# Top-k attention and two experts on one core: the softmax normaliser moved to GpSimd, a value product over two tiles, and all weight conversions of the second expert inside attention

## The chip, the core and the metric

The kernel runs on one core of a Trainium2 chip. The core has a matrix engine (TensorE, in the rows PE; PEld is its weight load), a vector engine (VectorE, DVE), a scalar engine (ScalarE, ACT), GpSimd (POOL), and SyncE (SP), whose queue issues every DMA of this kernel. On-chip memory is SBUF, and PSUM for what TensorE writes. Each engine runs its own instructions in the order in which they were written; engines wait for each other on semaphores. The metric is the device time of one execution in microseconds (us).

## What is computed

Attention over 4 batches, 8 heads, 576 positions and head size 64 keeps only the 32 highest scores of each row; its output goes through a gated expert and then a second one.

```python
def _attn_ref(q, k, v):                          # (4, 8, 576, 64)
    scores = scale * np.matmul(q, k.transpose(0, 1, 3, 2))
    kth = np.partition(scores, -32, axis=-1)[..., -32:-31]
    scores = np.where(scores >= kth, scores, -1e9)
    attn = np.exp(scores - np.max(scores, axis=-1, keepdims=True))
    attn = attn / (np.sum(attn, axis=-1, keepdims=True) + 1e-09)
    return np.matmul(attn, v)

def _moe_ref(x, w_gate, w_val, w_out):           # 2304 x 512, d_ff 1536
    g = x @ w_gate
    return (g * (1 / (1 + np.exp(-g))) * (x @ w_val)) @ w_out

def _moe2_ref(x, w_in, w_out):                   # d_ff 2048
    h = x @ w_in
    return (h * np.cos(h)) @ w_out
```

## The kernel before

**Tiling.** The 2304 tokens are 18 tiles of 128. They go in ten chunks c: chunks 0 and 1 of one tile, chunks 2 to 9 of two (`SIZES`). The heads go in four pairs p. A unit is one tile t of one head h: 144 units, in the order of chunk, pair, tile, head. A tile that crosses a batch boundary (tiles 4 and 13) has two segments of 64 rows with different keys and values.

**A unit (`unit_proc`).** TensorE makes 128x576 scores in PSUM (`sc`, L605), ScalarE copies them to a tile `s` (L610), VectorE finds the 32 largest by four rounds of a maximum of eight (`MAX8`, L633) and three of striking them out (`MATCH_REPLACE8`, L636). GpSimd makes two bounds from them (`b`, L647 and L651), ScalarE masks (L664) and takes the exponential with its row sum (`e`, `sm`, L675). The tile `s` stays taken until the masking is done; there are five (ring `r_s`).

**A pair of heads (`pair_proc`, `group_proc`).** TensorE transposes the exponentials of a tile's two heads (`tp`, L697), ScalarE copies them to `pt` (L702), and TensorE multiplies them with the values into `av`: one product with the tail of the values (L735) and eight with 64-column weights (L738), in full fp32, two records for each. That is done for each tile by itself. Value tiles `V` come by DMA (L568); there are three.

**The normaliser (`x_proc`).** When the row sums of a chunk and a pair of heads are there, VectorE adds 1e-9 (L759) and takes the reciprocal (L757), GpSimd spreads it (`rx`, L765), TensorE turns it (L777), ScalarE copies it and the value product, GpSimd multiplies them, and the chunk's input to the first expert is split in two fp32r parts `xh` and `xl`.

**The first expert.** For each chunk 12 blocks f of 128 hidden columns: `gv` = x times the gate and value weights (L884; for chunks 0 and 1 in plain fp32 with the operands turned, L973), silu on ScalarE and GpSimd, `y` = times the output weights (L1096), stored to DRAM. The last chunk's products are called `gvl`.

**Weights.** They come as 64-bit words, and `convert` makes fp32 of them: three ScalarE passes (L213, L216, L220), a join on VectorE (L223), an add on GpSimd (L226). The first expert's weights are then split into two fp32r parts (`w1_rest`, L300 and L303). Of the second expert's 16 blocks, 12 are converted during attention in halves (`w2_early_proc`) and stored to DRAM (`w2d`); the other four are loaded raw and converted after attention (`w2_proc`, tiles `w2s` and `cy`). All 16 are split when the first expert's weights give their room free (L1241, L1245).

**The second expert.** For 6 blocks j of 384 tokens and 16 blocks f: `h` (L1309, 12 products), its cosine product on ScalarE and VectorE, `o` (L1373, 9 products).

**What sets the order.** A planner (`Plan`) runs the steps as processes with a cost and a due time each and emits every engine's instructions in the order in which it would start them. A ring is a set of buffers: a step waits until the buffer that it reuses is free. So a changed cost or due time moves instructions all over the program.

## Time and profile before

| | us |
|---|---|
| median of 3 runs (lowest, highest) | 1283.73 (1279.42, 1286.16) |
| profiled execution | 1285.8 |
| its span | 1284.0 |
| TensorE busy | 1199.9 (93%) |
| VectorE busy | 1014.5 (79%) |
| ScalarE busy | 963.7 (75%) |
| GpSimd busy | 626.6 (49%) |

The profile is of one execution. Its span runs from the first to the last instruction; the profiled time has 1.8 us around it. Attention and the first expert take the time to about 800 us, the rest of the last chunk's first expert to about 870 us, the second expert the time from about 860 us to the end. The view of stretches gives each engine's busy time in a stretch, the timeline gives instructions with their start and length, the view of waits says who waited for whom, and the chain of waits goes back from the last instruction.

### The profile page before, as it was taken

Reading aid. Unit: us, or ns where it says so; the run is one execution under the profiler, and the core shown is the slowest. Engines: PE = TensorE matmul, PEld = TensorE weight load, DVE = VectorE, ACT = ScalarE, POOL = GpSimd, SP = SyncE. Lnnn points to the kernel's source line nnn. Section 1 sums busy time; section 2 is a strip of 40 time slices with the busy share of each in tenths; the row PEclk is TensorE's granted clock in tenths of the full one; section 3 lists DMA queues with packets and bytes.
Section 4 is the critical chain, followed back from the end, with each engine's and each line's share of the span. In section 5 each row is a group of like instructions: output and inputs, shape, how many; then the busy total and the mean of one; then the engine's idle time right before and its main releaser. Section 6 shows DMA issues by size and latency. Waiting matters only on the chain.

```text
span 1284.0 us, 24500 instructions
## 1 busy us (share of the span) xinstructions
PE 1199.9 (93%) x8544; PEld 1092.0 (85%) x8544; DVE 1014.5 (79%) x2024; ACT 963.7 (75%) x2164; POOL 626.6 (49%) x1039
## 2 busy tenths in 40 slices
PE   2588988999999999999999999998999999999998
PEld 1466765899998999999999999996999899899897
DVE  6999999999999999999999995256555555555554
ACT  6999999879898888888888877459554555455554
POOL 5556688978677767667666655456010101000000
PEclk9999989999999999999999999999999999999999
DMA  6553545555465654455545432784010101010000
GB/s 214 188 197 102 174 125 163 162 176 195 153 191 175 183 171 157 156 162 169 169 144 177 140 117 67 244 274 129 7 50 1 50 1 44 7 37 2 3 23 25
DMA packets 83099, 157.97 MB, mean 123 GB/s; under 512 B 16672, under 2 KB 35104, under 8 KB 82976
## 3 DMA queue, kind: packets, MB, share of 16 engines
q1 hardware_dynamic: 82976, 156.41, 38.3%
q8 instruction: 67, 1.10, 0.4%
q14 instruction: 56, 0.46, 0.1%
HBM read 131.20 MB, written 25.17 MB: 122 GB/s over the span
## 4 chain that ended last, share of the span: by engine, by line
PE 64%; DVE 12%; ACT 11%; DMA 5%; POOL 3%; issue 3%; SPq 1%; POOLq 0%; ACTq 0%; DVEq 0%
PE o L1373 15%; PE h L1309 15%; PE gv L884 11%; PE y L1096 8%; DVE m L633 6%; DVE w L636 5%; PE av L738 4%; PE sc L605 3%; PE tp L697 3%; PE gv L973 3%; DMA wo<-wo 1%; ACT pt L702 1%; PE gvl L884 1%; DMA y<-yo 1%; ACT s L610 1%
## 5 line engine op out<-in xcount | busy, mean ns | idle before, releaser
L633 DVE MAX8 m<-w 128x8 f32<-128x576 f32 x432 | 311.0, 745 | 1.2
L884 PE MATMUL gv<-xh,w 128*128 128x256 f32 x1344 | 289.1, 292 | 5.9 <-ACT hg L852 5.8
L884 PEld LDWEIGHTS gv<-xh,w 128*128 128x128 f32 x1344 | 224.4, 190 | 11.8 <-ACT hg L852 7.9
L1309 PE MATMUL h<-x2h,w 128*128 128x384 f32 x768 | 213.1, 338 | 4.8 <-DVE g L1343 4.8
L636 DVE MATCH_REPLACE8 w<-m,w 128x576 f32<-128x576 f32 x288 | 212.6, 739 | 0.0
L1373 PE MATMUL o<-w,gh 128*128 128x512 f32 x576 | 195.9, 395 | 0.0
L884 PE MATMUL gv<-xl,w 128*128 128x256 f32 x672 | 189.6, 282 | 0.0
L1096 PE MATMUL y<-gh,wo 128*128 128x256 f32 x768 | 159.2, 289 | 1.2 <-DMA wo<-wo 1.2
L605 PE MATMUL sc<-K,q 128*128 128x288 f32 (+1 forms) x640 | 126.6, 327 | 34.0 <-ACT s L610 14.6
L1309 PEld LDWEIGHTS h<-x2h,w 128*128 128x128 f32 x768 | 140.4, 188 | 11.1 <-DVE g L1343 7.0
L1276 POOL TENSOR_TENSOR x2l<-x,x2h 128x384 fp32r<-128x384 f32 x24 | 25.6, 1066 | 250.0 <-ACT x2h L1265 250.0
L1343 DVE TENSOR_TENSOR g<-r,h 128x384 f32<-128x384 f32 x96 | 53.2, 554 | 114.4 <-ACT r L1338 114.4
L605 PEld LDWEIGHTS sc<-K,q 128*128 128x128 f32 (+1 forms) x640 | 97.2, 197 | 44.9 <-ACT s L610 16.8
L1336 ACT ACTIVATE r<-r 128x384 f32<-128x384 f32 x96 | 50.4, 525 | 110.3 <-DVE r L1333 110.3
L702 ACT ACTIVATE pt<-tp 128x512 f32<-128x512 f32 (+1 forms) x216 | 107.1, 496 | 33.5 <-PE tp L697 32.3
L697 PE MATMUL tp<-ident,e 128*128 128x128 f32 x648 | 111.8, 283 | 21.8 <-ACT pt L702 18.1
L1096 PEld LDWEIGHTS y<-gh,wo 128*128 128x128 f32 x768 | 126.3, 190 | 5.7 <-issue 4.5
L1309 PE MATMUL h<-x2l,w 128*128 128x384 f32 x384 | 129.3, 337 | 0.0
L884 PEld LDWEIGHTS gv<-xl,w 128*128 128x128 f32 x672 | 127.9, 190 | 0.0
L1373 PEld LDWEIGHTS o<-w,gh 128*128 128x128 f32 x576 | 108.1, 188 | 21.0
L675 ACT ACTIVATE e<-e,b 128x576 f32<-128x576 f32 x144 | 112.9, 784 | 3.2 <-POOL b L651 1.4
L633 DVE MAX8 m<-s 128x8 f32<-128x576 f32 x144 | 107.3, 746 | 9.4 <-ACT s L610 6.2
(122 smaller groups left out, 2895.3 us busy)
## 6 DMA issues: line engine op xcount, KB each, us to landing
wo<-wo SPq DMA_DIRECT2D x96, 512.0 KB, 3.8
w_raw<-in_w SPq DMA_DIRECT2D x48, 512.0 KB, 4.8
V<-in_vP SPq DMA_DIRECT2D x52, 256.0 KB, 3.4
kx<-in_kT SPq DMA_DIRECT2D x64, 144.0 KB, 3.0
qx<-in_qT SPq DMA_DIRECT2D x64, 128.0 KB, 2.9
wo<-in_wo SPq DMA_DIRECT2D x12, 512.0 KB, 4.0
wo<-wo SPq DMA_DIRECT2D x24, 256.0 KB, 2.8
w2d<-c SPq DMA_DIRECT2D x24, 256.0 KB, 2.6
```

The source lines that it names most:

```text
L605: nc.tensor.matmul(sc[:r1, s, :HALF], q[:, a, t * 128:t * 128 + r1], k[:, s * HALF:s * HALF + HALF], start=a == 0, stop=a == 1)
L633: nc.vector.max(out=st["m"][:, 8 * i:8 * i + 8], in_=st["w"] if i else st["s"])
L636: nc.vector.match_replace(out=st["w"], in_to_replace=st["m"][:, 8 * i:8 * i + 8], in_values=st["w"] if i else st["s"], imm_value=LOWEST)
L675: nc.scalar.activation(st["e"], st["e"], AF.Exp, bias=st["b"][:, 2:3], scale=1.0, accum_out=smT[c, p][:, j:j + 1])
L697: nc.tensor.transpose(st["ps"][:, j - j0], e[:, j * 128:j * 128 + 128], ident)
L702: lambda: nc.scalar.activation(ptT[c, p, t][:, j0:j1], st["ps"][:, :j1 - j0], AF.Copy),
L738: nc.tensor.matmul(o[64 * h:64 * h + 64, r0:r1], m[:, j, h], pt[:, 5 * h + j, r0:r1], start=False, stop=j == 3)
L884: nc.tensor.matmul(gv[g], W1[f, kk // 2][:, a, g, kk % 2], m[:, kk], start=kk == 0 and i == 0, stop=kk == KT - 1 and i == 2)
L1096: nc.tensor.matmul(y1p[d // 2][:, d % 2], w[:, a, d * 128:d * 128 + 128], m, start=f == 0 and i == 0 and d % 2 == 0, stop=f == NF1 - 1 and ...
L1309: nc.tensor.matmul(st["h"], w[:, a, kk * 128:kk * 128 + 128], m[:, kk], start=kk == 0 and n == 0, stop=kk == KT - 1 and n == 2)
L1343: nc.vector.tensor_mul(st["g"], r, h)
L1373: nc.tensor.matmul(o[t], a[:, cs], W2[f, 1][:, m], start=f == 0 and n == 0, stop=f == NF2 - 1 and n == 2)
```

## The change

1. The normaliser's add and reciprocal go from VectorE to GpSimd. The reciprocal becomes a power of -1.
2. The value product is made once for a chunk's two tiles and a pair of heads (`av_proc`): `pt` is 256 columns wide for both tiles, and one product runs over 256 columns (or over 64 and 192 where a batch boundary lies in the chunk).
3. All 16 blocks of the second expert are converted during attention; those after attention go. `w2_proc` only loads and splits.
4. The splitting of the first expert's weights has an earlier due time (`W1S_FIRST` 96 for 122). Score tiles go from five to four, value tiles from three to two, tiles for the second expert's loaded weights (`cvx`) from five to nine.
5. The first 12 products `h` get a third PSUM bank, wait for their half of a weight block alone, and the first token block's input is due 50 us earlier.
6. Some of the planner's costs change: a strike 0.725 for 0.669 us, a transpose 0.108 for 0.09, the value product by the number of segments and tiles.

The code for turned chunks also gets branches for a last chunk of one tile; here the last chunk has two, so no instruction comes from them, and they are left out below.

```diff
-    NV = 3
+    NV = 2
-    W1S_FIRST, W1S_STEP = 122.0, 2.6
+    W1S_FIRST, W1S_STEP = 96.0, 2.7
...
     def w2_early_proc(i):
         f, half = divmod(i, 2)
-        due = due_unit(46 + 3.8 * i)
+        due = due_unit(44 + 2.9 * i)
...
-    r_s, r_sc, r_w, r_e, r_pt, r_tp, r_av = Ring(5), Ring(1), Ring(2), Ring(2), Ring(1), Ring(1), Ring(1)
+    r_s, r_sc, r_w, r_e, r_pt, r_tp, r_av = Ring(4), Ring(1), Ring(2), Ring(2), Ring(1), Ring(1), Ring(1)
...
-                yield "DVE", 0.669, strike, due, True
+                yield "DVE", 0.725, strike, due, True
...
-        end = yield "PE", 0.02 + 0.09 * (j1 - j0), turn, due, True
+        end = yield "PE", 0.02 + 0.108 * (j1 - j0), turn, due, True
...
-            ptT[c, p, t] = att.tile([128, 9, 128], F32, tag="pt", name="pt", bufs=r_pt.n)
+            if (c, p) not in ptT:
+                ptT[c, p] = att.tile([128, 9, CH], F32, tag="pt", name="pt", bufs=r_pt.n)[:, :, :SIZES[c] * 128]
...
+    def av_proc(c, p):
+        n = SIZES[c]
+        yield ev_pt[c, p]
+        segs = segments(FIRST[c], n)
+        for b, r0, r1 in segs:
+            yield ev_v[c, p, b]
+        yield r_av.gate(c * NP + p)
...
             for b, r0, r1 in segs:
                 m, tail = V[c, p, b]
-                nc.tensor.matmul(o[:, r0:r1], tail, pt[:, 4, r0:r1], start=True, stop=False)
+                nc.tensor.matmul(av[:, r0:r1], tail, pt[:, 4, r0:r1], start=True, stop=False)
                 for j in range(4):
                     for h in range(2):
-                        nc.tensor.matmul(o[64 * h:64 * h + 64, r0:r1], m[:, j, h], pt[:, 5 * h + j, r0:r1],
+                        nc.tensor.matmul(av[64 * h:64 * h + 64, r0:r1], m[:, j, h], pt[:, 5 * h + j, r0:r1],
                                          start=False, stop=j == 3)
-        end = yield "PE", 1.1, attv, due_unit(u) + 15.0, True
+        end = yield "PE", 0.34 * len(segs) + 1.13 * n, attv, due_unit(unit_of[c, p, n - 1, 1]) + 15.0, True
...
         def rinv():
             sm = smT[c, p]
-            nc.vector.reciprocal(sm, sm)
-
-        yield ("DVE", 0.07, lambda: nc.vector.tensor_scalar(smT[c, p], smT[c, p], 1e-9, None, op0=OP.add), due,
+            nc.gpsimd.tensor_tensor(sm, sm, cst[:, 2:2 + 2 * n], op=OP.pow)
+
+        yield ("POOL", 0.15, lambda: nc.gpsimd.tensor_scalar(smT[c, p], smT[c, p], 1e-9, None, op0=OP.add), due,
                True)
-        yield "DVE", 0.1, rinv, due, True
+        yield "POOL", 0.2, rinv, due, True
...
-    r_raw2, r_cvx2, r_x2, r_x2s = Ring(2), Ring(5), Ring(2), Ring(2)
+    r_cvx2, r_x2, r_x2s = Ring(9), Ring(2), Ring(2)
+    r_hc = Ring(1)
...
     def w2_proc(i):
...
-        if f < NS2:
-            yield w2_stored[f]
-            yield r_cvx2.gate(i)
...
-        else:
-            pc = pools["pbc"]
...
-            joined, t = yield from convert(
-                st["raw"].bitcast(I32), due, [r_cy2.gate(n)],
-                lambda: pools["psB"].tile([128, DM], I32, tag="cy", name="cy", bufs=r_cy2.n), into)
...
+        yield w2_stored[f]
+        yield r_cvx2.gate(i)
+
+        def load():
+            st["x"] = pools["pbc"].tile([128, DM], F32, tag="cvx", name="cvx", bufs=r_cvx2.n)
+            nc.sync.dma_start(st["x"], w2d[f, :, half * DM:half * DM + DM])
...
-        due = b_due(j, 0) - 25.0
+        due = b_due(j, 0) - (25.0 if j else 75.0)
...
-        yield ev_w2[f]
+        yield ev_w2[f, 0]
         yield ev_x2[j]
-        second = k >= H_ONE and k % 2
+        if k < H_ONE:
+            second, third, i = False, k % 3 == 2, k // 3 if k % 3 == 2 else k // 3 * 2 + k % 3
...
+                elif third:
+                    st["h"] = pools["psB"].tile([128, DM], F32, tag="h", name="h")[:, :CB]
...
-    for i in range(2 * NS2):
+    for i in range(2 * NF2):
         plan.start(w2_early_proc(i))
```

How the order of instructions changes is shown at three places, in which a name after an arrow is what is read. The first is the normaliser of chunk 6, head pair 1 (`sm` holds the row sums, `b` a unit's bounds, `rx` the spread normaliser, `gl` a part of the first expert). On VectorE before, its add and reciprocal stand between the selections of two units:

```order
L633 MAX m<-w 128x8
L759 TENSOR_SCALAR sm<-sm 128x4
L636 MATCH_REPLACE w<-m,s 128x576
L636 MATCH_REPLACE w<-m,w 128x576
L757 RECIPROCAL sm<-sm 128x4
L633 MAX m<-w 128x8 x2
```

On GpSimd now, both stand between a unit's bounds and the spread:

```order
L941 TENSOR_TENSOR vv<-th,vv 128x256
L651 TENSOR_TENSOR b_6723<-b_6723 128x1
L763 TENSOR_SCALAR sm<-sm 128x4
L761 TENSOR_TENSOR sm<-sm,cst 128x4
L951 TENSOR_TENSOR gl_6743<-vv,gh_6742 128x256
L769 TENSOR_SCALAR rx<-sm 128x256
L647 TENSOR_TENSOR b_6803<-m,cst 128x2
```

The two steps left VectorE and stand on GpSimd ahead of the next unit's bounds. The second place is TensorE at a value product of the same chunk (`gv` belongs to the first expert). Before, for one tile:

```order
L884 MATMUL gv_100<-xh,w_3_1991 128x256
L735 MATMUL av<-pt,vtail_105 128x128
L738 MATMUL av<-pt,V 64x128 x8
L884 MATMUL gv_100<-xh,w_3_1991 128x256
L884 MATMUL gv_100<-xl,w_3_1991 128x256
```

Now, for both tiles, right behind the turned normaliser:

```order
L781 MATMUL tp<-ident,rx 128x128 x2
L740 MATMUL av<-pt,vtail_107 128x256
L743 MATMUL av<-pt,V 64x256 x8
L889 MATMUL gv_100<-xh,w_5_1833 128x256
L889 MATMUL gv_100<-xl,w_5_1833 128x256
```

Two narrow blocks became one wide block. The third place is TensorE where the second expert's first products `h` stand among the last chunk's `gvl`; the number behind `w_` is the block f of the first expert. Before:

```order
L884 MATMUL gvl<-xl,w_10_2488 128x256
L884 MATMUL gvl<-xh,w_10_2488 128x256
L1309 MATMUL h<-x2h,w_0_11689 128x384
L1309 MATMUL h<-x2l,w_0_11689 128x384
L1309 MATMUL h<-x2h,w_0_11689 128x384
L884 MATMUL gvl<-xh,w_11_2541 128x256
```

Now:

```order
L889 MATMUL gvl<-xl,w_5_1833 128x256
L889 MATMUL gvl<-xh,w_5_1833 128x256
L1363 MATMUL h<-x2h,w_0_11495 128x384
L1363 MATMUL h<-x2l,w_0_11495 128x384
L1363 MATMUL h<-x2h,w_0_11495 128x384
L889 MATMUL gvl<-xh,w_6_1870 128x256
```

The first `h` moved from behind block 10 to behind block 5 of the last chunk.

## Rows read from the trace of the kernel before

**Rows 1.** Stretches: start:end, length, busy us (instructions), TensorE's granted clock, DMA share

```profile
core 0: us, PE busy (x) PEld busy (x) DVE busy (x) ACT busy (x) POOL busy (x), PEclk, DMA share, GB/s
100.00:200.00 100.00, 89.98 (x529) 66.56 (x528) 99.34 (x209) 96.11 (x222) 69.87 (x115) 0.95 0.44 136
200.00:240.00 40.00, 33.12 (x255) 25.28 (x253) 40.00 (x85) 35.97 (x80) 36.06 (x49) 1.00 0.51 157
240.00:790.00 550.00, 538.72 (x4842) 517.78 (x4841) 538.00 (x1115) 473.23 (x1139) 389.56 (x707) 1.00 0.51 161
840.00:905.00 65.00, 58.24 (x380) 53.12 (x379) 41.29 (x63) 48.53 (x99) 37.84 (x30) 1.00 0.55 181
905.00:1284.00 379.00, 375.32 (x1875) 338.43 (x1874) 198.73 (x357) 201.64 (x390) 16.26 (x16) 1.00 0.06 20
```

**Rows 2.** Timeline: start, length, engine, line; copy and first maximum, units 30 and 48

```profile
181.32 0.69 ACT L610 ACTIVATE s<-sc 128x576 f32<-128x576 f32 x1
...
187.01 0.74 DVE L633 MAX8 m<-s 128x8 f32<-128x576 f32 x1
...
278.08 0.65 ACT L610 ACTIVATE s<-sc 128x576 f32<-128x576 f32 x1
...
278.83 0.76 DVE L633 MAX8 m<-s 128x8 f32<-128x576 f32 x1
```

**Rows 3.** Waits of VectorE, 240 to 790 us: total us, times, longest

```profile
DVE m L633 <- ACT s L610: 5.7, 9, 1.5
DVE m L633 <- POOL th L935: 2.9, 2, 1.9
```

**Rows 4.** VectorE's timeline at a normaliser; then L759's durations (ns min/median/max)

```profile
503.75 0.47 DVE L759 TENSOR_SCALAR sm<-sm 128x4 f32<-128x4 f32 x1
504.13 0.08 DVE L636 MATCH_VALUE_LOAD w<-m,s 128x8 f32 x1
...
505.59 0.16 DVE L757 RECIPROCAL sm<-sm 128x4 f32<-128x4 f32 x1
505.67 0.72 DVE L633 MAX8 m<-w 128x8 f32<-128x576 f32 x1
...
L759 DVE TENSOR_SCALAR sm<-sm x40: 139/388/1319, 34.9 to 793.4; 128x4 f32<-128x4 f32 x32, 128x2 f32<-128x2 f32 x8
```

**Rows 5.** Groups of GpSimd: count | busy us, mean ns | idle before, releasers

```profile
L647 POOL TENSOR_TENSOR b<-m,cst 128x2 f32<-128x2 f32 x144 | 30.1, 210 | 86.5 <-DVE m L633 71.0 <-DVE sm L757 7.5 <-DVE sm L759 4.8
```

**Rows 6.** Line 223, the joins from 260 to 760 us: ns min/median/max, first, last

```profile
L223 DVE SCALAR_TENSOR_TENSOR w_raw<-w_raw,c x24: 658/846/1651, 262.9 to 736.0; 128x512 int32<-128x512 int32 x24
```

**Rows 7.** TensorE's timeline at a whole and at a cut value product

```profile
504.30 0.38 PE L735 MATMUL av<-pt,vtail 128*128 128x128 f32 x2
504.61 1.09 PE L738 MATMUL av<-pt,V 128*64 128x128 f32 x16
505.64 0.39 PE L884 MATMUL gv<-xh,w 128*128 128x256 f32 x1
...
581.16 0.33 PE L735 MATMUL av<-pt,vtail 128*128 128x64 f32 x2
...
583.02 0.38 PE L1096 MATMUL y<-gh,wo 128*128 128x256 f32 x1
```

**Rows 8.** Chain of waits near 100 us: start, us, what

```profile
98.53 4.99 PE gv L973 x22
103.51 0.44 PE tp L697 x4
```

**Rows 9.** Waits of SyncE's queue, whole span: total us, times, longest

```profile
SPq L568 <- PE av L738: 74.8, 29, 7.8
```

**Rows 10.** Chain of waits, one of the passes between 866 and 898 us

```profile
890.82 0.56 ACT w2s L216
```

**Rows 11.** Waits of TensorE, 790 to 905 us

```profile
PE h L1309 <- DVE g L1343: 4.8, 5, 2.7
```

**Rows 12.** Line 633, the maxima: ns min/median/max, start of the first and last

```profile
L633 DVE MAX8 m<-w x432: 722/744/765, 15.6 to 788.4; 128x8 f32<-128x576 f32 x144
```

More of the change, by code (lines that the diff above doesn't have):

```diff
@@ L32 @@
 NCH = len(SIZES)
-TURNED = [c < PLAIN for c in range(NCH)]
+TURNED = [n == 1 for n in SIZES]
 FIRST = [sum(SIZES[:c]) for c in range(NCH)]
@@ L963, in turned_gemm_proc @@
         due = moe_due(c, 2 * fp)
+        last = c == NCH - 1
         if fp:
@@ L994, in turned_gemm_proc, with tiles @@
-        ring.free(i, end, plan)
-        th, hg, vv = st["th"], st["hg"], st["vv"]
-        yield ("POOL", 0.37,
-               lambda: nc.gpsimd.tensor_scalar(th, th, 1.0, 0.5, op0=OP.add, op1=OP.mult), due, True)
-        yield "POOL", 0.69, lambda: nc.gpsimd.tensor_mul(th, th, hg), due, True
-        end = yield "POOL", 0.69, lambda: nc.gpsimd.tensor_mul(vv, th, vv), due, True
+        gate, val = bank[:, :, 0], bank[:, :, 1]
+        def tiles(*names):
+            for name in names:
+                st[name] = moe.tile([128, CH], F32, tag=name, name=name, bufs=(r_vv if name == "vv" else r_th).n)
@@ new lines, in tanh, with silu, product @@
+        def tanh():
+            tiles("th")
+            nc.scalar.activation(two("th"), gate, AF.Tanh, scale=0.5)
+        def evac():
+            tiles("hg", "vv")
+            nc.scalar.activation(two("hg"), gate, AF.Copy)
+            nc.scalar.activation(two("vv"), val, AF.Copy)
+        def silu():
+            tiles("vv")
+            nc.vector.scalar_tensor_tensor(two("vv"), two("th"), 1.0, gate, op0=OP.add, op1=OP.mult)
+        def product():
+            nc.vector.scalar_tensor_tensor(two("vv"), two("vv"), 0.5, val, op0=OP.mult, op1=OP.mult)
@@ L1000, in turned_gemm_proc @@
+        vv = st["vv"]
         r_th.free(k, end, plan)
[L1001 removed]
+        stored = not last and fp < NG0
         if not stored:
[L1003 to L1009 removed]
+            yield r_g.gate(G0[c] + (fp if last else fp - NG0))
+        if last:
+            yield r_gt.gate(fp)
+        else:
+            kt = tp_count[0]
+            tp_count[0] += 1
+            yield r_tp.gate(kt)
@@ L1047, in turned_wout_proc @@
                 wo0_free(f, end)
-        r_x.free(c, end, plan)
+        if not last:
+            r_x.free(c, end, plan)
         due = moe_due(c, NF1)
@@ L1177, in pool_c_proc @@
     def pool_c_proc():
-        for f in range(NF2):
-            yield ev_w2[f]
+        for event in ev_w2.values():
+            yield event
         def swap():
```

211 lines of the change are left out of this document (118 added, 93 removed).

## The prediction

> **What bounds the kernel now.** I read the busy times of the engines in stretches first, since the shares of the whole span mix four different jobs. In [rows 1] the reader is to see where two engines are full at once. From 100 to 240 us VectorE is full (99.34 of 100, then 40.00 of 40) and ScalarE nearly (96.11 of 100), while TensorE idles 10 and 7 us: selection paces. From 240 to 790 us TensorE is busy 538.72 of 550 and VectorE 538.00: both are full. From 905 us TensorE alone counts; nothing in the change touches what it does there.
>
> Which of the two paces the middle is not in busy times. I take it from the order of two neighbours in the timeline: when a unit's scores are copied out of PSUM, and when its first maximum starts. Early, the copy is done at 182.01 and the maximum starts at 187.01: 5 us of stock. Later the copy ends at 278.73 and the maximum starts 0.10 us on [rows 2]. VectorE is then waiting for the copy (5.7 us in nine waits, and 2.9 us in two more put down to a product on GpSimd) [rows 3]. So from 240 us the scores arrive just in time, TensorE's queue sets when, and VectorE sits right behind it. A gain on one of them alone is given back in the middle; a gain on both counts.
>
> After attention, TensorE idles 6.8 us of the 65 from 840 to 905 us, where ScalarE is busy 48.53 us [rows 1]: the last weights are converted there, and the first nonlinear work of the second expert stands in the same queue.
>
> **The normaliser.** The add and the reciprocal leave VectorE 40 times. What they cost it is the advance to the next instruction, 503.75 to 504.13 and 505.59 to 505.67: 0.46 us together, 18.4 us over the run [rows 4]. On GpSimd they become an add and a power on the same small tile. The trace has no power. Nearest is the product of 128x2, mean 210 ns [rows 5], which also is a floor; I take 0.2 us for the add and 0.3 us for the power, 20 us of GpSimd in all, where it idles 160 us from 240 to 790 us [rows 1]. An upper end does not exist in the rows; the last rival below says from which price it would hurt. The add waits for the last exponential of its block, and what queues behind it on GpSimd are the next unit's threshold operations, for which ScalarE's masking waits; 5 us of score stock covers that early, little later, and I put no more than 2 us on it.
>
> How long the add took on VectorE is a story of its own: 139 ns at least, 388 at the median, 1319 at most [rows 4]. The Trainium skill (Advanced Engine Details and Errata, VectorE Performance Modes) says that VectorE's second SBUF port is shared with GpSimd, so that instructions of both block each other. The spread in the row agrees, and the rule also speaks against the change: the joins of the conversion have two inputs, and GpSimd gets busier. It is the third rival.
>
> **Eight more conversions in attention.** Each brings three ScalarE passes, a join on VectorE and an add on GpSimd, a load and a store. The join takes 846 ns at the median there, 658 at least [rows 6]: 8 x 0.85 = 6.8 us on VectorE. Net, VectorE loses 11.6 us of work before 790 us. ScalarE gets 24 passes of about 0.55 us, 13 us, into 550 us of which it uses 473 [rows 1]: covered there. Less covered is the other move: the splitting of the first expert's weights comes 9 passes (5 us) earlier, into the stretch before 240 us where ScalarE has 4 us to spare per 100.
>
> **The value product.** A block of one tile runs from 504.30 to 505.64: 1.34 us, of which 0.31 for the two records of the tail and 1.03 for sixteen narrow ones, which run two at a time. A block cut by a batch boundary, two halves of 64 columns, runs from 581.16 to 583.02: 1.86 us, 0.93 a half [rows 7]. From 64 to 128 columns a half block grows by 0.41 us, so by that line 256 columns take 1.34 + 0.82 = 2.16 us, against 2 x 1.34 = 2.68 now. That is one end; 2.68 (each record twice as long) is the other. Between them stands the full-precision product with 256 columns in the first chunks: 22 records in 4.99 us, 0.227 us each [rows 8], which gives 16/2 x 0.227 + 2 x 0.227 = 2.27 us, and some 0.1 us for changing over. I take 2.35, since that row is the same arithmetic at the same width: 0.33 us saved for each of 24 whole pairs. For the 8 pairs with a cut, 1.86 + 1.34 = 3.20 now becomes 0.93 + 1.75 (192 columns on the line), 0.5 us less. Sum 8 + 4 = 12 us of TensorE, 10 of them after 240 us, where it paces.
>
> **Buffers.** Score tiles go from five to four, value tiles from three to two. A copy then waits for the masking of the unit four back; early there are 5 us of stock, and I bound the price by VectorE's present wait for copies, 0 to 6 us [rows 3]. SyncE already waits for value products before it loads new values (74.8 us in 29 waits) [rows 9]; with one tile fewer such a load starts later, and the loads behind it in that queue too, but the product that needs it is some 20 us (four units) away. I take nothing for it and keep 2 us for the range.
>
> **The transition.** Between 840 and 905 us eight conversions vanish: 24 ScalarE passes (one of them 0.56 us of the chain [rows 10], so 13 us), 8 joins, 8 adds. The chain of waits runs through just these passes there, and the second expert's first products wait for its nonlinear work (4.8 us of TensorE in five waits) [rows 11]. The first products of the second expert now also stand among the last gate products, with their inputs loaded earlier and a third PSUM bank. Of the 6.8 us of idle I take back 5. The bounds are 0 (another wait behind it, on inputs that come no sooner) and 7.
>
> **The sum.** Before 240 us VectorE saves 14 normalisers x 0.46 = 6.4, less one join, 5.5 us; ScalarE is given 5 us more in the same stretch. I take half, 2.5 (bounds 0 and 5.5). In the middle TensorE saves 10, and VectorE must save as much: 26 x 0.46 - 7 x 0.85 = 6, and its 8.6 us of waits cover the rest. The transition gives 5. Together 17.5 us. The profiled execution took 1285.8 us around a span of 1284.0, so 1268.3; the median of the runs, 1283.73, lies 2.1 lower, so **1266**.
>
> **Rivals.**
> First, the wide product saves nothing: the records are twice as long, 2.68 us a pair. Then the middle keeps its length, and 2.5 + 5 remain: 1276. For it: sixteen records in 1.03 us are 64 ns each, not far above half of the 110 ns at which full-width records of 128 columns follow each other (four transposes in 0.44 us [rows 8]). Against it: the cut blocks show a part that does not grow with columns.
>
> Second, ScalarE fills up. It is at 96.11 of 100 already from 100 to 200 us and gets 5 us more there, and 13 us in the middle. Then nothing is gained before 240 us and some 5 us are lost in the middle to scores that are copied late: 1266 + 2.5 + 5 = 1274.
>
> Third, the joins get slower with a busier GpSimd. If the 30 joins of the middle take 1.3 us (half way from the median to the longest, 1651 ns [rows 6]), VectorE gets 30 x 0.45 = 13.5 us back, more than the 6 it saved; the middle then keeps its length: 1276. By the rule of the Trainium skill named above this is what GpSimd's added work does.
>
> Fourth, everything at its good end: 5.5 before 240 us, the product at 2.16 (14 us in the middle), 7 in the transition, together 26.5: 1257.
>
> Fifth, slower: the power on GpSimd is dear. GpSimd has 160 us idle in the middle; the added joins' adds and the 26 adds take 12, which leaves 5.7 us for each of 26 powers. From there GpSimd paces, and every further microsecond costs 26. At 7 us a power, the middle grows by 34 us instead of shrinking by 10: 1310. For it: no row of a power. Against it: four elements a partition, and the smallest products on GpSimd all take about 0.2 us [rows 5].
>
> **How the numbers follow.** The sum 0.50 (its own range 1258 to 1272), no gain from the wide product 0.12, ScalarE full 0.12, slower joins 0.06, everything good 0.13, dear power 0.07. The range goes from the fourth rival's neighbourhood to beyond the first: 1253 to 1281; the fifth is left out, and the tails of the fourth. A difference under 0.5% (6.4 us) is about what a measurement of this kernel can't tell from none. Faster by more than that: the sum, the fourth, the second, and half of the first and third, 0.82; within it 0.10; slower 0.08.
>
> **What would show it.** Right: VectorE's last maximum moves from 788.4 us [rows 12] to about 776; blocks of the wide product take about 2.35 us from their first record to the next product; the time from the start of the last maximum to the end, 495.6 us, falls by about 5; the wait of the first products of the second expert disappears. Wrong: a power of several microseconds with idle ScalarE behind it; ScalarE above 97% from 100 to 240 us with VectorE waiting for copies; joins above 1.2 us; gaps on VectorE ahead of each first maximum in the middle as now or longer, which would say that TensorE's queue still sets the pace and that what I took from the product was not there.

## The result, and the profile after

The changed kernel took 1302.72 us (median of 4 runs, 1301.21 to 1304.28) beside 1283.62 us of the kernel before (four runs by now): ratio 1.0140, 95% interval 1.0120 to 1.0159. It is 1.4% slower, 37 us above the forecast and 22 us above the top of its range. The profiled execution took 1304.28 us around a span of 1302.5.

The stretches of the kernel after, with the columns of [rows 1] (busy us and count of each engine, granted clock, DMA share):

```profile
core 0: us, PE busy (x) PEld busy (x) DVE busy (x) ACT busy (x) POOL busy (x), PEclk, DMA share, GB/s
100.00:200.00 100.00, 80.83 (x430) 58.49 (x429) 97.77 (x198) 96.97 (x221) 80.77 (x131) 0.95 0.38 120
200.00:240.00 40.00, 35.59 (x197) 24.31 (x197) 34.58 (x71) 32.66 (x73) 28.47 (x44) 0.96 0.56 170
240.00:790.00 550.00, 522.77 (x4328) 485.22 (x4328) 518.64 (x1036) 468.34 (x1129) 417.39 (x738) 1.00 0.54 171
811.40:863.00 51.60, 47.19 (x386) 44.30 (x386) 12.91 (x20) 25.56 (x64) 29.35 (x37) 1.00 0.54 178
863.00:928.00 65.00, 62.36 (x415) 59.22 (x415) 40.61 (x61) 37.37 (x78) 25.57 (x19) 1.00 0.49 162
```

Two stretches got worse. From 100 to 200 us TensorE idles 19.2 us where it idled 10.0, and VectorE, which was full from 200 to 240 us, is busy 34.58 of the 40 [rows 1]; from 240 to 790 us TensorE idles 27.2 us (11.3 before) and VectorE 31.4 (12.0 before). Neither of the two engines that were full is full any more: something else holds both. It is not TensorE's clock: from 240 us on the granted clock is 1.00 in both kernels. It is lower only earlier (0.57 from 50 to 75 us, so partly at the lower of the two levels, where it was 1.00 before), while VectorE paces, and no time is lost there: unit 24 starts its selection at 154.7 us, before the change at 155.1.

The last maximum says where the time was lost (line 633: shortest/median/longest in ns, first and last start):

```profile
L633 DVE MAX8 m<-w x432: 731/747/765, 15.2 to 811.4; 128x8 f32<-128x576 f32 x144
```

It moved from 788.4 us [rows 12] to 811.4, 23.0 later; from there to the end it is 491.1 us instead of 495.6. So attention lost 23 us, 4.9 of them by the start of unit 44 (263.0 us for 258.1) and the rest later. Behind the last maximum 4.5 us came back. The transition has to be compared at the same distance from the last maximum, which is what the last two stretches above are; the first of them was before

```profile
788.40:840.00 51.60, 49.65 (x422) 47.38 (x421) 11.97 (x23) 25.93 (x64) 24.97 (x33) 1.00 0.59 199
```

and the second is the stretch from 840 us of [rows 1]. In the second, ScalarE's 48.53 us are 37.37, the wait of [rows 11] is gone, and TensorE idles 2.6 us instead of 6.8. In the first it idles 4.4 instead of 1.9 (3.0 of it in one wait for a DMA of output weights). From the last maximum to the end its idle time falls by 1.6 us in all; the other 2.9 of the 4.5 are work that TensorE had already done by then.

What holds the two engines stands in the waits from 240 to 790 us (total us, times, longest). First the kernel before, then the kernel after:

```profile
ACT th L851 <- POOL vv L936: 5.8, 6, 2.1
PE gv L884 <- ACT hg L852: 5.1, 6, 1.5
PE y L1096 <- POOL gl L946: 0.7, 3, 0.3
```

```profile
ACT th L856 <- POOL vv L941: 20.8, 23, 1.7
DVE m L633 <- ACT s L610: 17.2, 22, 3.2
PE gv L889 <- ACT hg L857: 10.0, 13, 1.6
PE y L1167 <- POOL gl L951: 6.0, 14, 1.0
```

The silu of the first expert goes around three engines: ScalarE writes `th`, GpSimd multiplies it in three instructions up to `vv`, and there is one buffer for `th`. ScalarE's next tanh waits for GpSimd's last product, TensorE's next gate products wait for ScalarE to empty their bank, and the scores behind them in TensorE's queue reach VectorE late. All four waits grew. GpSimd is the one waited for, with 133 us idle in the same stretch. Where it idles is seen from its groups there (count | busy us, mean ns | idle before, who ended it):

```profile
L951 POOL TENSOR_TENSOR gl<-vv,gh 128x256 fp32r<-128x256 f32 x76 | 57.0, 750 | 37.4 <-ACT gh L947 23.5 <-issue 12.0 <-POOL b L651 1.0
L647 POOL TENSOR_TENSOR b<-m,cst 128x2 f32<-128x2 f32 x100 | 20.6, 206 | 19.8 <-DVE m L633 19.6
L939 POOL TENSOR_SCALAR th<-th 128x256 f32<-128x256 f32 x75 | 31.8, 424 | 2.2 <-ACT th L856 1.5
```

It waits for ScalarE's copy of a silu and for VectorE's maxima, but hardly at all ahead of a silu's first product (L939, 2.2 us in 75): when a silu comes, GpSimd is at something else. Even with no power ahead, the first product starts 1.8 us behind its tanh at the median.

The normaliser on GpSimd (same columns as the maxima above; L761 is the power, L763 the add):

```profile
L761 POOL TENSOR_TENSOR sm<-sm,cst x40: 710/1032/1047, 34.8 to 818.4; 128x4 f32<-128x4 f32 x32, 128x2 f32<-128x2 f32 x8
L763 POOL TENSOR_SCALAR sm<-sm x40: 223/228/622, 34.5 to 817.7; 128x4 f32<-128x4 f32 x32, 128x2 f32<-128x2 f32 x8
```

The add is what was assumed (0.23 us for 0.2), the power more than three times what was (1.03 for 0.3).

### The profile page after: what moved, and what is told of

Read it like the earlier page. It is cut to its first block, busy times and chain, and to the rows that moved or that the text cites. A ratio compares the mean times of both kernels' runs of the same rounds, so it can differ in the third digit from the quotient of the medians.

```text
span 1302.5 us, 23598 instructions
## 1 busy us (share of the span) xinstructions
PE 1196.6 (92%) x8040; PEld 1070.1 (82%) x8040; DVE 1006.2 (77%) x1945; ACT 958.2 (74%) x2164; POOL 673.2 (52%) x1118
## 3 DMA queue, kind: packets, MB, share of 16 engines
q8 instruction: 63, 1.03, 0.3%
## 4 chain that ended last, share of the span: by engine, by line
PE 46%; ACT 20%; POOL 12%; DVE 9%; DMA 6%; issue 5%; SPq 1%; POOLq 0%; ACTq 0%; DVEq 0%
PE o L1428 15%; PE h L1363 15%; PE y L1167 4%; DVE m L633 4%; DVE w L636 4%; PE gv L889 4%; ACT e L675 3%; ACT e L664 2%; PE gvl L889 2%; ACT pt L703 2%; ACT s L610 2%; DMA w_raw<-in_w 2%; PE av L743 2%; POOL sm L761 1%; POOL K L496 1%
## 5 line engine op out<-in xcount | busy, mean ns | idle before, releaser
L889 PE MATMUL gv<-xh,w 128*128 128x256 f32 x1344 | 287.1, 292 | 10.7 <-ACT hg L857 10.7
L1167 PE MATMUL y<-gh,wo 128*128 128x256 f32 x768 | 156.3, 286 | 5.4 <-DMA wo<-wo 4.1
L1167 PEld LDWEIGHTS y<-gh,wo 128*128 128x128 f32 x768 | 125.3, 190 | 10.1 <-issue 4.1
L633 DVE MAX8 m<-s 128x8 f32<-128x576 f32 x144 | 107.9, 751 | 27.2 <-ACT s L610 23.1
L697 PEld LDWEIGHTS tp<-ident,e 128*128 128x128 f32 x648 | 80.6, 146 | 50.4 <-ACT pt L703 40.5
```

What stands on the lines that cost most here:

```text
L633: nc.vector.max(out=st["m"][:, 8 * i:8 * i + 8], in_=st["w"] if i else st["s"])
L697: nc.tensor.transpose(st["ps"][:, j - j0], e[:, j * 128:j * 128 + 128], ident)
L889: nc.tensor.matmul(gv[g], W1[f, kk // 2][:, a, g, kk % 2], m[:, kk], start=kk == 0 and i == 0, stop=kk == KT - 1 and i == 2)
L1167: nc.tensor.matmul(y1p[d // 2][:, d % 2], w[:, a, d * 128:d * 128 + 128], m, start=f == 0 and i == 0 and d % 2 == 0, stop=f == NF1 - 1 and ...
```

## Experiments

Each was timed beside the kernel before, whose median was 1284.2 to 1284.7 us; the ratio and its interval behind each time are to that kernel. They come in the order of the questions; a line of dots in an edit or a view stands for lines left out.

### Is it the length of the power?

**e1_mult** keeps the kernel after and its order on every engine, and puts a product by 0.001 where the power was (so the row sums are scaled, not inverted).

```diff
-    nc.vector.memset(cst[:, 2:6], -1.0)
+    nc.vector.memset(cst[:, 2:6], 0.001)
-            nc.gpsimd.tensor_tensor(sm, sm, cst[:, 2:2 + 2 * n], op=OP.pow)
+            nc.gpsimd.tensor_tensor(sm, sm, cst[:, 2:2 + 2 * n], op=OP.mult)
```

> The changed kernel with a product by 0.001 in the place of the power, so the normaliser's value is not the reference's; every engine has the same instructions in the same order. Theory P (the power's length): the power takes 1.03 us where its place in the order was planned for 0.2 us, GpSimd comes late to the first expert's silu, ScalarE's next tanh waits for it, and TensorE for ScalarE; with a product of about 0.2 us that goes, 1270 to 1284. Rival Q (one score tile and one value tile fewer, and the other order) and rival R (eight more conversions in attention): both stay, 1296 to 1303.

**e5_pow2** goes the other way: a second power, by 1.0 (what columns 6 to 9 of `cst` then hold), behind each first one.

```diff
             nc.gpsimd.tensor_tensor(sm, sm, cst[:, 2:2 + 2 * n], op=OP.pow)
+            nc.gpsimd.tensor_tensor(sm, sm, cst[:, 6:6 + 2 * n], op=OP.pow)
```

> The kernel after with a second power (by 1.0) behind each of the 40 first ones; the order on every engine is that of the kernel after, one GpSimd instruction added at each place. P (GpSimd's length passes through the single tanh tile to ScalarE and TensorE): the first power's surplus over a product, 32 x 0.84 + 8 x 0.52 = 31 us of GpSimd, was worth 14 us; the second one puts 32 x 1.03 + 8 x 0.71 = 39 us more there, so 17 to 25 us more, 1318 to 1330, and ScalarE's wait for GpSimd's products above the 20.8 us of the kernel after. R (the 14 us came from something else in how the power executes, once per place): within 4 us of the kernel after, 1299 to 1307. T (GpSimd is hurt only from the threshold of the prediction's fifth rival, 5.7 us a power): no change either, 1299 to 1307.

Measured: 1288.59 us (1.0031, 1.0018 to 1.0045) with the product, 1302.72 with one power, 1340.06 (1.0433, 1.0410 to 1.0456) with two. The instruction in e1_mult, then the second power in e5_pow2:

```profile
L761 POOL TENSOR_TENSOR sm<-sm,cst x40: 194/202/646, 34.5 to 803.3; 128x4 f32<-128x4 f32 x32, 128x2 f32<-128x2 f32 x8
```

```profile
L763 POOL TENSOR_TENSOR sm<-sm,cst x40: 697/1018/1269, 35.1 to 858.4; 128x4 f32<-128x4 f32 x32, 128x2 f32<-128x2 f32 x8
```

The first power is longer than the product by 32 x 0.83 + 8 x 0.53 = 31 us and cost 14; the second is 32 x 1.02 + 8 x 0.71 = 38 us and cost 37. So nearly half of the first surplus went straight through to the end, and all of the second. With the product the kernel stands between the range for the power as the whole loss (1270 to 1284) and that of the others (1296 to 1303): the power is most of the loss, not all that kept the gain away. The range for e5_pow2 was too low, in the direction of the theory; the theories by which nothing should have happened fall. The waits go with the dose; in e1_mult, then in e5_pow2 (whose lines stand one or two later):

```profile
ACT th L856 <- POOL vv L941: 12.7, 18, 1.7
...
PE gv L889 <- ACT hg L857: 3.3, 7, 0.8
```

```profile
ACT th L858 <- POOL vv L943: 29.0, 21, 2.5
PE gv L891 <- ACT hg L859: 19.1, 14, 2.7
```

One place shows it link by link, in the kernel after (start, length, engine, line; at the end of a line the idle time before it and who ended it):

```profile
300.42 0.74 POOL L940 TENSOR_TENSOR th<-th,hg 128x256 f32<-128x256 f32 x1
...
301.12 1.03 POOL L761 TENSOR_TENSOR sm<-sm,cst 128x4 f32<-128x4 f32 x1
...
302.12 0.73 POOL L941 TENSOR_TENSOR vv<-th,vv 128x256 f32<-128x256 f32 x1
...
302.88 0.38 ACT L856 ACTIVATE th<-gv 128x256 f32<-128x256 f32 x1 [1.24 <-POOL vv L941]
...
303.59 0.39 PE L889 MATMUL gv<-xh,w 128*128 128x256 f32 x1 [1.04 <-ACT hg L857]
...
304.93 0.76 DVE L633 MAX8 m<-s 128x8 f32<-128x576 f32 x1 [0.47 <-ACT s L610]
```

The same instructions in e1_mult:

```profile
299.95 0.20 POOL L761 TENSOR_TENSOR sm<-sm,cst 128x4 f32<-128x4 f32 x1
...
300.11 0.74 POOL L941 TENSOR_TENSOR vv<-th,vv 128x256 f32<-128x256 f32 x1
...
300.88 0.38 ACT L856 ACTIVATE th<-gv 128x256 f32<-128x256 f32 x1 [0.54 <-POOL vv L941]
...
301.59 0.39 PE L889 MATMUL gv<-xh,w 128*128 128x256 f32 x1 [0.34 <-ACT hg L857]
```

The power is 0.83 us longer than the product; ScalarE's idle time grows by 0.70 us, TensorE's by 0.70, and VectorE's next first maximum, which followed at once in e1_mult, waits 0.47. Of 33 powers from 100 to 800 us this one alone stands between two products of such a silu; 25 stand between two silus, often as a block of add, power and spread, and 7 come before the first of them. That they delay the silu behind them shows when ScalarE's wait for `vv` is counted apart, from 240 to 790 us: behind silus that have a power ahead of them or in them it is 2.4 us with the product, 10.7 with one power and 22.0 with two; behind all other silus it is 10.4, 10.1 and 7.0.

**e2_dve_same_plan** puts both instructions back on VectorE at the same places, every other engine's order untouched.

```diff
-            nc.gpsimd.tensor_tensor(sm, sm, cst[:, 2:2 + 2 * n], op=OP.pow)
+            nc.vector.reciprocal(sm, sm)
-        yield ("POOL", 0.15, lambda: nc.gpsimd.tensor_scalar(smT[c, p], smT[c, p], 1e-9, None, op0=OP.add), due,
+        yield ("POOL", 0.15, lambda: nc.vector.tensor_scalar(smT[c, p], smT[c, p], 1e-9, None, op0=OP.add), due,
```

> The changed kernel with the add and the reciprocal back on VectorE, at the places where the planner had put them; ScalarE, TensorE and SyncE keep their order word for word. P: GpSimd loses all 1.26 us a normaliser, VectorE gets back 0.46 us (18 us, half of it hidden by its waits): 1270 to 1288. Q and R: VectorE has more to do and nothing else changes, 1300 to 1312.

1293.45 us (1.0076, 1.0051 to 1.0101), between the ranges. In one and the same order VectorE's relief is worth 1293.45 - 1288.59 = 4.9 us when GpSimd takes it over with two short instructions, of the 18.4 us that leave VectorE.

**h3_powcost** changes no work and tells the planner what the trace says of the two instructions.

```diff
-        yield ("POOL", 0.15, lambda: nc.gpsimd.tensor_scalar(smT[c, p], smT[c, p], 1e-9, None, op0=OP.add), due,
+        yield ("POOL", 0.23, lambda: nc.gpsimd.tensor_scalar(smT[c, p], smT[c, p], 1e-9, None, op0=OP.add), due,
...
-        yield "POOL", 0.2, rinv, due, True
+        yield "POOL", 1.03, rinv, due, True
```

> The kernel after with the planner told what the two instructions of the normaliser take in the trace (0.23 and 1.03 us for 0.15 and 0.20); the work is the same, the order is planned anew. O (the loss is one of order: the planner puts the power where it has no room): 1286 to 1296. P (the loss is GpSimd's work that must stand between two silu products wherever it is put): 1297 to 1306.

1285.37 us (1.0000, 0.9984 to 1.0016): 17 us less than the kernel after, with the same instructions, and just below the range for a loss of order. The loss was one of placing: planned at 0.2 us, a power was put ahead of work that had no 0.8 us to spare. In h3_powcost ScalarE's wait for GpSimd's products is half (same stretch as above):

```profile
ACT th L856 <- POOL vv L941: 10.0, 14, 1.5
...
PE gv L889 <- ACT hg L857: 3.8, 8, 0.8
```

### How much is an order worth by itself?

**n1_jitter_h4** and **n2_jitter_before** change the price of a strike, as told to the planner, by 3 ns: in h4_noadd (below) and in the kernel before. No work changes, the order of all engines does.

```diff
-                yield "DVE", 0.725, strike, due, True
+                yield "DVE", 0.722, strike, due, True
```

```diff
-                yield "DVE", 0.669, strike, due, True
+                yield "DVE", 0.672, strike, due, True
```

> h4_noadd with one cost told to the planner changed by 3 ns (a strike 0.722 for 0.725 us): the work is the same, the order is another one. If the 13 us gained by h4_noadd belong to its work: 1266 to 1276. If they are the luck of one order among many: anything from 1266 to 1290, and the differences of 5 to 10 us between other kernels here say little.

> The kernel before with the same 3 ns (0.672 for 0.669 us). Its distance from the kernel before, with no work changed, is a measure of what any newly planned order is worth: under 3 us either way if orders hardly matter, up to 10 us if the five kernels built on the kernel before that came out 4 to 11 us slower were slower for their order.

1275.30 us (0.9921, 0.9904 to 0.9939) beside 1270.99 of h4_noadd, and 1289.78 us (1.0039, 1.0026 to 1.0052) beside 1284.25 of the kernel before. So 4 and 6 us come from nothing but the order (two samples). The kernel before is the better of its two orders, and a difference of up to some 6 us between kernels planned apart says nothing of their work. The comparisons below are read with that; the 17 us of h3_powcost, also planned apart, are well above it.

### What are the other parts worth?

**e4_dve** is the kernel after with the normaliser on VectorE, planned there as before.

```diff
-        yield ("POOL", 0.15, lambda: nc.gpsimd.tensor_scalar(smT[c, p], smT[c, p], 1e-9, None, op0=OP.add), due,
+        yield ("DVE", 0.07, lambda: nc.vector.tensor_scalar(smT[c, p], smT[c, p], 1e-9, None, op0=OP.add), due,
...
-        yield "POOL", 0.2, rinv, due, True
+        yield "DVE", 0.1, rinv, due, True
```

> The changed kernel with the normaliser back on VectorE, planned as before the change: the wide value product, the conversions in attention and the transition alone. P: 1262 to 1280, faster than before by the product and the transition. Q and R: 1295 to 1310.

1284.12 us (0.9996, 0.9985 to 1.0007), above the 1262 to 1280 of the power as the whole loss and below the 1295 to 1310 of its rivals: without the power the rest of the change loses nothing, but gains nothing either.

**e3_before_pow** is the kernel before with the normaliser on GpSimd alone, at the planner's prices of the change.

```diff
-            nc.vector.reciprocal(sm, sm)
+            nc.gpsimd.tensor_tensor(sm, sm, cst[:, 2:2 + 2 * n], op=OP.pow)
...
-        yield "DVE", 0.1, rinv, due, True
+        yield "POOL", 0.2, rinv, due, True
```

> The kernel before with the normaliser's move to GpSimd alone (add and power, planned as in the change). P: the loss is there without the rest, 1298 to 1312. Q and R: VectorE is relieved of 18 us and nothing else is touched, 1272 to 1284.

1289.30 us (1.0042, 1.0022 to 1.0061), between the ranges, and within half a microsecond of the kernel before in its other order (1289.78). There the power's length and VectorE's relief cancel or neither counts; the run doesn't tell which.

**g3_before_buf** takes the buffers alone, **g2_before_wide** the wide product with them (and the changed price of a transpose), both on the kernel before.

```diff
-    NV = 3
+    NV = 2
-    r_s, r_sc, r_w, r_e, r_pt, r_tp, r_av = Ring(5), Ring(1), Ring(2), Ring(2), Ring(1), Ring(1), Ring(1)
+    r_s, r_sc, r_w, r_e, r_pt, r_tp, r_av = Ring(4), Ring(1), Ring(2), Ring(2), Ring(1), Ring(1), Ring(1)
```

```diff
+    def av_proc(c, p):
+        n = SIZES[c]
+        yield ev_pt[c, p]
+        segs = segments(FIRST[c], n)
...
-        end = yield "PE", 1.1, attv, due_unit(u) + 15.0, True
+        end = yield "PE", 0.34 * len(segs) + 1.13 * n, attv, due_unit(unit_of[c, p, n - 1, 1]) + 15.0, True
```

> The kernel before with four score tiles for five and two value tiles for three, and nothing else. B: slower, 1289 to 1298. V and W: as before, 1281 to 1287.

> The kernel before with the wide value product alone (and what its room costs: four score tiles, two value tiles). W: the product's own 8 us come through, 1274 to 1279. B and V: they do not, 1283 to 1294.

1290.55 us (1.0037, 1.0019 to 1.0055) and 1295.64 us (1.0081, 1.0058 to 1.0103). The first lies in the range for buffers that cost, 1289 to 1298, but 0.8 us from the kernel before in its other order: it can't be told from an order. The second lies above all its ranges: the wide product gained nothing in that plan; if anything it lost.

**g4_narrow** is the reverse: e4_dve with the product of the kernel before, its buffers and its price of a transpose.

```diff
-    NV = 2
+    NV = 3
...
-        end = yield "PE", 0.34 * len(segs) + 1.13 * n, attv, due_unit(unit_of[c, p, n - 1, 1]) + 15.0, True
+        end = yield "PE", 1.1, attv, due_unit(u) + 15.0, True
```

> The changed kernel with the normaliser on VectorE and the value product of single tiles, five score tiles and three value tiles as before: what is left is all conversions in attention, the early splits and the transition. B and V: the transition's 5 us come through, 1276 to 1281. W: the early crowding eats them, 1284 to 1292.

1285.42 us (1.0007, 0.9992 to 1.0022), 1.3 above e4_dve: no difference. The wide product does take work off TensorE, which is busy 1193.5 us in the profile of e4_dve and 1205.7 in that of g4_narrow; but it idles 89 us there and 80 here, so most of the 12 us (the blocks themselves explain 8, as worked out below) come back as waits.

**g1_w1s_late** is e4_dve with the first expert's splits due as before.

```diff
-    W1S_FIRST, W1S_STEP = 96.0, 2.7
+    W1S_FIRST, W1S_STEP = 122.0, 2.6
```

> The changed kernel with the normaliser on VectorE (run e4, 1284 us) and the first expert's splits due late again, as before the change. Theory W (early splits and more conversions crowd ScalarE before 300 us, where the units fell 6 us behind): 1274 to 1280. Theories B (a score tile and a value tile fewer) and V (the wide product waits for both tiles of a pair, and TensorE has it in one lump): 1281 to 1288.

1281.66 us (0.9979, 0.9964 to 0.9994), 2.5 less than with the early splits, by itself within what an order is worth, and not in the range of the theory that they are the loss (1274 to 1280).

### Does a gain need more than one engine?

The row sum contains the exponential of the row's maximum, so it is at least 1 and in fp32 adding 1e-9 changes nothing. That gives a relief of VectorE without a new instruction anywhere: leaving the add out and keeping the reciprocal on VectorE. **h4_noadd** does it in g1_w1s_late, **k1_before_noadd** in the kernel before, **m4_before_wide_noadd** in g2_before_wide. The edit is the same in all three:

```diff
-        yield ("DVE", 0.07, lambda: nc.vector.tensor_scalar(smT[c, p], smT[c, p], 1e-9, None, op0=OP.add), due,
-               True)
```

> The kernel after with the normaliser on VectorE, without the add of 1e-9 (the row sum is at least 1, so the add changes nothing in fp32), and with the first expert's splits due as before. V (VectorE's relief is worth its length in the middle): the add is 0.38 us 40 times, 15 us, 26/40 of it in the middle, so 1270 to 1276 against the 1281.7 of the same kernel with the add. M (TensorE, ScalarE and GpSimd pace the middle together and VectorE follows): within 4 us, 1278 to 1285.

> The kernel before without the add of 1e-9 alone: only the VectorE relief of the prediction's first part, 40 x 0.38 = 15 us, and nothing put on another engine. V: 5 to 12 us faster, 1272 to 1279. M (VectorE's relief is given back, since TensorE's queue brings the scores): within 4 us of the kernel before, 1280 to 1288.

> The kernel before with the wide product (four score and two value tiles) and without the add: both engines relieved, and neither the conversions nor the transition touched. B: some 10 us below g2_before_wide (1295.6), 1281 to 1288. F (the gain of h4_noadd belongs to the other parts of the change, conversions and transition): 1292 to 1298.

h4_noadd: 1270.99 us (0.9894, 0.9869 to 0.9919), the best of all, and 10.7 below g1_w1s_late. k1_before_noadd: 1289.08 us (1.0029, 1.0011 to 1.0046), 0.7 from the kernel before in its other order: nothing, where 5 to 12 us were expected if VectorE's relief counted alone. m4_before_wide_noadd: 1289.31 us (1.0033, 1.0021 to 1.0046), 6.3 below g2_before_wide but no gain on the kernel before, just above the range that stood for "both engines relieved".

**m1_narrow_noadd** takes the wide product out of h4_noadd (the edit is that of g4_narrow), **m2_noadd_early** gives it the early splits back, and **m3_powcost_late** is h3_powcost with late splits, so the whole change with both repairs.

```diff
-    W1S_FIRST, W1S_STEP = 122.0, 2.6
+    W1S_FIRST, W1S_STEP = 96.0, 2.7
```

> h4_noadd with the value product made for each tile by itself, five score tiles and three value tiles: VectorE is relieved by 40 adds, TensorE isn't. B (middle paced by two engines, a gain on one is given back): 1280 to 1287, as g4_narrow (1285.4), which also has the adds and the early splits. A (the adds alone are the 11 us between g1_w1s_late and h4_noadd): 1270 to 1276.

> h4_noadd with the first expert's splits due as early as in the change (96 for 122), nothing else. E (the early splits cost ScalarE its room before 240 us, as 2.5 us between e4_dve and g1_w1s_late said): 1272 to 1278. N (they cost nothing once VectorE has room): 1269 to 1272.

> The kernel after with both repairs: the planner knows the power's price, and the first expert's splits are due as before. TensorE has its 8 us less and VectorE its 18 us less. B (both relieved, so the gain shows wherever the normaliser went): 1268 to 1277. G (GpSimd's 50 us more of work take back through ScalarE what VectorE gains): 1280 to 1286.

1277.70 us (0.9949, 0.9929 to 0.9969), 1281.08 (0.9974, 0.9965 to 0.9984) and 1284.54 (0.9987, 0.9969 to 1.0006). Against the two orders of h4_noadd (1270.99 and 1275.30): taking away the wide product costs 2 to 7 us, the early splits 6 to 10, the add 6 to 11, and the normaliser on GpSimd instead of a lone reciprocal on VectorE 9 to 14. Only the last is clear of what an order is worth at both ends, and it contains the add: beside g1_w1s_late, which has add and reciprocal on VectorE, m3_powcost_late is 2.9 us slower, which says nothing.

The stretches from 100 to 200 and from 240 to 790 us of h4_noadd, m2_noadd_early and m3_powcost_late, in this order:

```profile
100.00:200.00 100.00, 87.70 (x467) 60.85 (x466) 99.79 (x209) 95.22 (x220) 68.98 (x114) 0.97 0.45 138
240.00:790.00 550.00, 538.40 (x4496) 504.75 (x4494) 530.83 (x1093) 486.73 (x1174) 396.38 (x717) 1.00 0.55 174
```

```profile
100.00:200.00 100.00, 84.31 (x429) 59.19 (x428) 97.75 (x200) 95.60 (x217) 76.39 (x119) 0.91 0.39 122
```

```profile
240.00:790.00 550.00, 532.66 (x4431) 497.99 (x4431) 527.38 (x1063) 481.99 (x1160) 424.60 (x763) 1.00 0.55 173
```

h4_noadd brings TensorE's idle time in the middle back to 11.6 us, as it was before, with a shorter product in it. With the early splits (m2_noadd_early) VectorE is no longer full from 100 to 200 us (97.75 for 99.79) and gets 200 instructions in for 209, in the stretch where selection paces. ScalarE's passes for the splits there (line 300: count | busy us, mean ns | idle before), in h4_noadd and in m2_noadd_early:

```profile
L300 ACT ACTIVATE w<-w_raw 128x512 fp32r<-128x512 f32 x13 | 9.2, 704 | 0.7 <-POOL w L303 0.7
```

```profile
L300 ACT ACTIVATE w<-w_raw 128x512 fp32r<-128x512 f32 x19 | 14.0, 735 | 0.0
```

Six passes more, 5 us of an engine that is 95% busy there, between score copies and masks of the same queue. In m3_powcost_late GpSimd works 28 us more in the middle than in h4_noadd, and TensorE and VectorE both idle more.

The form in which a gain counts only on both engines isn't confirmed. m1_narrow_noadd has TensorE's old product and is faster than the kernel before; m4_before_wide_noadd has both reliefs and isn't. Besides the product and the add, what separates them are the conversions during attention, the transition and the planner's prices of a strike and a transpose; which of these lets the gain through stays open. A second buffer for the tanh, which would test the coupling of the three engines directly, wasn't tried.

## Why the prediction was wrong, step by step

Of the 37 us between forecast and measurement 14 are the power's length in the order of the change. Without it (e1_mult) the kernel is still 23 us above the forecast, since the gains taken before 240 us and in the middle didn't come.

**The power, first failed step.** "I take 0.2 us for the add and 0.3 us for the power": the add is 0.23, the power 1.03 (0.72 on two elements a partition). The nearest row was a product on a tile as small, and size was taken for price; the operation was another one. The range 1253 to 1281 had no room for it, since only a price from 5.7 us was thought to hurt. As placed, the surplus cost 14 us.

**The threshold, second failed step.** "GpSimd has 160 us idle in the middle ... which leaves 5.7 us for each of 26 powers. From there GpSimd paces". A sum of idle time is no reserve unless it lies where the new instruction is put. GpSimd idles where it waits for ScalarE's copies and VectorE's maxima; ahead of a silu it has nothing to spare, and a power put there delays ScalarE, then TensorE, then VectorE. At a quarter of idle time, 0.46 us of each added microsecond already reached the end, and with the second power 0.98. The fifth rival had the right instruction and not the mechanism: GpSimd never ran out of time (133 us idle), it came late; in the order of the change 1.03 us already hurt, less than a fifth of 5.7.

**The placing, a step that was missing.** The prediction costed instructions and took the order for given. The change told the planner 0.2 us for a power of 1.03, and h3_powcost shows that this mismatch, not the work, was the 17 us, give or take the 4 to 6 of any new order.

**Before 240 us.** "I take half, 2.5 (bounds 0 and 5.5)": the sign was wrong. TensorE idles 9 us more from 100 to 200 us, VectorE is less full, ScalarE is at 96.97, and unit 44 starts 4.9 us late. The second rival named the place, at 2.5 us. That the early splits are the cause isn't shown: they cost 6 to 10 us in m2_noadd_early, but 1 and 2.5 in the pairs h3_powcost and m3_powcost_late, e4_dve and g1_w1s_late, and n2_jitter_before, which has late splits and only another order, starts unit 44 at 266.0, 7.9 us late.

**The value product.** The width was read rightly, a boundary was overlooked. A whole block of 256 columns, from its first record to the next product, in the kernel after; then one of chunk 5, whose two tiles belong to two batches:

```profile
508.15 0.60 PE L740 MATMUL av<-pt,vtail 128*128 128x256 f32 x2
508.68 1.95 PE L743 MATMUL av<-pt,V 128*64 128x256 f32 x16
510.56 0.39 PE L889 MATMUL gv<-xh,w 128*128 128x256 f32 x1
```

```profile
421.52 0.39 PE L740 MATMUL av<-pt,vtail 128*128 128x128 f32 x2
421.84 1.09 PE L743 MATMUL av<-pt,V 128*64 128x128 f32 x16
422.87 0.49 PE L740 MATMUL av<-pt,vtail 128*128 128x128 f32 x2
423.28 1.09 PE L743 MATMUL av<-pt,V 128*64 128x128 f32 x16
424.31 0.38 PE L889 MATMUL gv<-xh,w 128*128 128x256 f32 x1
```

The first takes 2.41 us (2.35 taken, so 0.27 saved for 0.33). In chunk 5 the batches meet between the two tiles, so its four products run as two halves of 128 columns and save nothing (2.78 us for 2.68); that makes 20 whole pairs, not 24. The eight cut pairs with 64 and 192 columns take 2.85 us (the first from 243.38 to 246.23) for 3.20, not 2.68. Together 20 x 0.27 + 8 x 0.35 = 8 us instead of 12. The first rival (nothing saved) is out: TensorE does have less to do.

**The middle.** "a gain on both counts" was the argument for 10 us there. Both engines did get less to do, and h3_powcost and m3_powcost_late still stand at 1285, within 1.3 and 2.9 us of the same kernels with the normaliser on VectorE (e4_dve, g1_w1s_late). In one and the same order the relief of VectorE was worth 4.9 of its 18.4 us (e1_mult beside e2_dve_same_plan). That the rest was given back because GpSimd, which took the work over, is in the same chain fits the waits and isn't shown: h4_noadd, with no new instruction on GpSimd, did gain 9 to 13 us on the kernel before, but k1_before_noadd and m4_before_wide_noadd, with the same relief, gained nothing. Why both counts were not enough stays open.

**Right, in part by luck.** The transition: 5 us of TensorE's idle time taken back, 4.1 measured in the 65 us in question (6.8 to 2.6). That the whole time from the last maximum to the end also falls by 4.5 is luck: 2.5 us of idle came in just ahead, and 2.9 us less work was left. Over the whole of it TensorE idles 1.6 us less, and 3 to 4 us less in e1_mult, e4_dve and h4_noadd. The buffers: 0 taken, nothing that can be told from an order. The joins, the third rival, didn't get slower; their row from 260 to 780 us in the kernel after:

```profile
L223 DVE SCALAR_TENSOR_TENSOR w_raw<-w_raw,c x30: 673/694/1232, 261.5 to 761.9; 128x512 int32<-128x512 int32 x30
```

694 ns at the median for 846 [rows 6], with GpSimd busier. The Trainium skill (Advanced Engine Details and Errata, VectorE Performance Modes) has VectorE's two-port instructions and GpSimd's block each other at a port that they share. The trace shows such blocking (last section), but not the loss that was worked out from it: in the new order 11 of 30 joins take more than 0.75 us, where it was 13 of 24.

## What to carry to other kernels

Idle time of an engine is a reserve only if nobody waits for what stands behind the new instruction; look at where the idle time lies, ahead of which instruction, and where other engines wait for what comes next cost an added instruction at its full length before looking at busy shares. Price an operation by a row of that operation, and give the planner the price that the trace shows: the same instructions were 17 us apart. Before a few microseconds are put down to a change, plan the kernel once more with a price moved by nothing: here 4 to 6 us came from the order alone.

## What the hardware showed that was not expected

A power on GpSimd takes 1035 ns on 128x4 and 721 on 128x2 (medians of 32 and 8), with an exponent of -1 as of 1 (1018 and 706 in e5_pow2), where a product takes 202 and 195. So it grows by about 0.16 us for each element of a partition (an estimate from the two rows), while the product hardly grows: the price lies in the operation, even on four elements.

Some instructions of VectorE stand still while GpSimd works. In the kernel before, the normaliser's add on VectorE takes 139 to 158 ns in the eight cases in which GpSimd runs nothing meanwhile; each of the 21 that take 383 ns or more ends within 30 ns of the end of an instruction of GpSimd, as the add of [rows 4], from 503.75 to 504.22, does with

```profile
503.45 0.74 POOL L946 TENSOR_TENSOR gl<-vv,gh 128x256 fp32r<-128x256 f32 x1 [0.95 <-ACT gh L942]
```

The joins behave alike: each of the 13 that take more than 0.75 us between 240 and 790 us starts while GpSimd runs an instruction and ends 0.54 to 0.57 us after it. The longest:

```profile
409.69 1.44 POOL L497 TENSOR_TENSOR K<-kx,K 64x576 fp32r<-64x576 f32 x1
410.03 1.65 DVE L223 SCALAR_TENSOR_TENSOR w_raw<-w_raw,c 128x512 int32<-128x512 int32 x1
```

So most of what the add cost VectorE was waiting for GpSimd, and the spread of the add's times, left as a story of its own in the prediction, has this cause. That is seen in when they end; no run was made for it.
